# In the last two wide blocks, layer 2 of half the tokens in seven products, with summed output weights through DRAM

## The chip, the cores and the metric

The kernel runs on one core of a Trainium2 chip. The metric is the device time of one execution in microseconds; lower is better. The kernel before took 1020.27 us (median of three runs, 1020.24 to 1021.65).

## The reference

Attention with random features, then a two-layer network over the 4608 tokens that come out of it, all in fp32:

```python
def phi(x):                       # x scaled by 64 ** -0.25
    proj = np.einsum('bhsd,md->bhsm', x, omega)
    h = proj - np.sum(x * x, axis=-1, keepdims=True) / 2.0
    return np.exp(h - np.max(h, axis=-1, keepdims=True)) / np.sqrt(m)
...
kv = np.einsum('bhsm,bhsd->bhmd', k_p, v);  z = np.sum(k_p, axis=2)
num = np.einsum('bhsm,bhmd->bhsd', q_p, kv)
den = np.einsum('bhsm,bhm->bhs', q_p, z)[..., None] + 1e-06
x = (num / den).transpose(0, 2, 1, 3).reshape(4608, 512)
...
h = x @ w_in                                         # 512 x 2048
g = np.where(h > 0, h, np.exp(np.minimum(h, 0)) - 1)  # ELU
out = g @ w_out                                      # 2048 x 512
```

There are 8 batches, 8 heads, 576 positions, 64 columns per head and 128 random features.

## The kernel before, in words

**Accuracy.** TensorE works on a reduced fp32 type, so every operand is kept as a high part and a low part (`xh`/`xl`, `w2h`/`w2l`, the two halves of a `gq` tile), and every product takes three matmuls: high by high, high by low, low by high.

**Stages.** Attention for pairs of heads runs beside the network: tokens that are finished go to DRAM (`xd`) and are fetched for the network when they are due. The network has 16 groups of 128 hidden features. The first 3072 tokens are done in blocks of 384: per group, layer 1 (L966 to L968), ELU (L975 to L987), layer 2 (L1000 to L1002). The last 1536 tokens are done in three **wide blocks** s = 0, 1, 2 of 512 tokens. A wide block has eight steps j, each for a pair of feature groups f = 2j and 2j + 1. Each step calls `fetch`, `wide1` and `wide2`.

**Layer 1 of a wide block** (`wide1`) takes seven products in place of eight (Strassen's method in Winograd's form over halves of the features, the inputs and the tokens). One product is six matmuls of 256 columns (L1223). Two PSUM banks called A and B collect them: A takes products 0, 5, 6 and 3 one on top of the other, and between them its partial sums are copied out to SBUF as c1, c2 and c3 (line 373 on ACT or 375 on DVE). B takes 1, 4 and 2, and its sums are added to these copies (L1246, DVE). The four results go through ELU (L1261 and L1266 on ACT, L1269 on DVE) and are split into `gq` tiles, a high part (copy, line 373 or 375) and a low part (subtraction, line 378, POOL or DVE). The two banks have one tag, "ph", with two slots, so A and B of a step take the slots that A and B of the step ahead give back.

**Layer 2 of a wide block** (`wide2`) is eight groups of three matmuls of 512 columns per step (L1312 to L1314), into one accumulator bank for each 128 tokens: `acc0` to `acc2` and one bank of the tag "pa". After the last step ACT copies each bank out (line 373) and SP stores it (L1327).

**Weights.** Layer 1 reads its weights from DRAM each step: three tiles `wp` of 512 KB (tag "w1c", three slots, L1191) and a half one, `wq` (L1196). Since a step uses all three slots, a `wp` load waits until TensorE has finished with the tile of the same number of the step ahead. The weights that Strassen's method needs summed are made ahead of time by `prepare` (L1036 to L1067), loaded as `rw`, summed on POOL, DVE and ACT, and stored to DRAM (`w1t`); some of them are made during block 0. The weights of layer 2 stay in SBUF.

**Order.** `Plan.order` is a list scheduler with costs, latencies, due times and buffer slots of its own; it fixes the order of the instructions on each engine when the program is built, and `Plan.issue` writes them in that order. SP issues all DMAs, strictly in its order, and waits for the condition of each before it goes on to the next. Constants at the head of the file set the due times and preferences (`STEP_S`, the length it assumes for a step; `LAG2`, how far layer 2 follows layer 1; `FETCH`, how early weights are due; `ALT`, which engine an operation may be given to).

## Time and profile before

| | us |
|---|---|
| median of three runs (device time) | 1020.27 |
| the profiled execution, device time | 1025.54 |
| its span, first to last instruction | 1023.8 |
| PE busy | 1002.9 |
| DVE busy | 743.4 |
| ACT busy | 708.0 |
| POOL busy | 542.2 |
| layer 1, blocks of 384: matmuls of L966, L967, L968, 512 each | 176.8, 172.7, 172.8 |
| layer 2, blocks of 384: matmuls of L1000, L1001, L1002, 384 each | 154.6, 151.3, 151.6 |

All times in the trace are microseconds from the start of the span. PE is TensorE's matmuls, PEld its weight loads, which have a track of their own. Matmuls are pipelined: the record of one is longer than the distance to the next, so that rates are read from distances between starts. In the profile a row of the view of lines is the engine's operation with "out<-in" by the names of the program, a count, busy time and the mean of one; rows of the timeline give start, duration, engine, line, operation, and in brackets the engine's idle time before it with what ended it. The three wide blocks stand at the end, from about 765 us on.

### The profile page before, as it was taken

To read this page: it belongs to the slowest core of one execution; us is meant where nothing else is said; L and a number is where in the kernel's file an instruction comes from. 1 tells how busy PE (TensorE), PEld (TensorE's weight loads), DVE (VectorE), ACT (ScalarE), POOL (GpSimd) and SP (SyncE) were. 2 spreads that over 40 slices of the span, in tenths; PEclk is the share of its full clock that TensorE was granted. 3 is DMA by queue.
4 is the path that set the end of the run, shared out by engine and by line. 5 is a ranking of instruction groups with operands and counts; after the bars stand their busy time and mean duration, and the time that the engine had idled before them with its cause. 6 is when DMAs were issued, how large, how long until landed. Compare 5 with 4: busy or idle time off the path is not lost. (4 is left out here: it accounts for less than half of the span.)

```text
span 1023.8 us, 23048 instructions
## 1 busy us (share of the span) xinstructions
PE 1002.9 (98%) x7374; PEld 882.3 (86%) x7374; DVE 743.4 (73%) x2799; ACT 708.0 (69%) x1879; POOL 542.2 (53%) x727
## 2 busy tenths in 40 slices
PE   7999999989999999999999999999999999999998
PEld 6888798878888888888888888888888989898897
DVE  5999977876778878888887888787675674345332
ACT  5999777777568788897788878875335555345443
POOL 0667676676457767776676766663003333323232
PEclk7999999999999999999999999999999999999999
DMA  6657677857766766676666867647979976666562
GB/s 172 184 182 217 233 265 251 256 175 238 236 244 200 228 221 218 201 250 201 218 220 201 250 186 231 204 153 213 332 269 346 311 276 205 197 204 194 192 183 82
DMA packets 91720, 226.17 MB, mean 221 GB/s; under 512 B 23056, under 2 KB 31952, under 8 KB 91600
## 3 DMA queue, kind: packets, MB, share of 16 engines
q1 hardware_dynamic: 91600, 224.70, 67.6%
q8 instruction: 59, 0.97, 0.4%
q14 instruction: 61, 0.50, 0.1%
HBM read 187.43 MB, written 37.22 MB: 219 GB/s over the span
## 5 line engine op out<-in xcount | busy, mean ns | idle before, releaser
L966 PE MATMUL ph<-xh,w1c 128*128 128x384 f32 x512 | 176.8, 345 | 5.7 <-DVE g L987 3.9
L967 PE MATMUL ph<-xl,w1c 128*128 128x384 f32 x512 | 172.7, 337 | 1.0 <-DVE xl L791 1.0
L968 PE MATMUL ph<-xh,w1c 128*128 128x384 f32 x512 | 172.8, 337 | 0.0
L378 POOL TENSOR_TENSOR gq<-y,gq 128x256 fp32r<-128x256 f32 x96 | 78.3, 832 | 171.3 <-ACT gq L373 97.7
L1000 PE MATMUL acc<-w2h,g 128*128 128x512 f32 x384 | 154.6, 403 | 0.1
L1002 PE MATMUL acc<-w2h,g 128*128 128x512 f32 x384 | 151.6, 395 | 0.0
L1001 PE MATMUL acc<-w2l,g 128*128 128x512 f32 x384 | 151.3, 394 | 0.0
L966 PEld LDWEIGHTS ph<-xh,w1c 128*128 128x128 f32 x512 | 96.6, 189 | 16.5 <-DVE g L987 6.6
L378 POOL TENSOR_TENSOR hq<-hq,den 128x512 f32<-128x512 f32 (+1 forms) x96 | 81.1, 853 | 46.2 <-DVE den L733 40.0
L967 PEld LDWEIGHTS ph<-xl,w1c 128*128 128x128 f32 x512 | 96.7, 189 | 4.0 <-DVE xl L791 1.4
L979 DVE SCALAR_TENSOR_TENSOR ph<-e,ph 128x384 f32<-128x384 f32 x128 | 71.2, 556 | 38.3 <-ACT e L976 37.5
L968 PEld LDWEIGHTS ph<-xh,w1c 128*128 128x128 f32 x512 | 96.6, 189 | 0.0
L975 ACT ACTIVATE e<-ph 128x384 f32<-128x384 f32 x128 | 62.6, 489 | 44.2 <-PE ph L968 43.0
L1002 PEld LDWEIGHTS acc<-w2h,g 128*128 128x128 f32 x384 | 72.1, 188 | 17.1
L724 DVE CUSTOM_DVE_ANT_0 junk<-hq,pz 128x128 f32<-128x128 f32 (+1 forms) x320 | 74.4, 279 | 15.7 <-PE pz L702 13.5
L1000 PEld LDWEIGHTS acc<-w2h,g 128*128 128x128 f32 x384 | 72.1, 188 | 15.7 <-issue 6.2
L375 DVE COPY c<-A 128x256 f32<-128x256 f32 x64 | 27.2, 425 | 74.2 <-PE A L1223 74.2
L458 ACT ACTIVATE hk<-hk,nbk 128x128 f32<-128x128 f32 x216 | 68.4, 390 | 17.2 <-POOL nbk L564 16.8
L1001 PEld LDWEIGHTS acc<-w2l,g 128*128 128x128 f32 x384 | 72.2, 188 | 8.1
L378 POOL TENSOR_TENSOR tk<-xk,tk 64x576 fp32r<-64x576 f32 x44 | 62.7, 1425 | 29.4 <-ACT tk L373 13.4
L458 ACT ACTIVATE hq<-hq,nbq 128x128 f32<-128x128 f32 x216 | 68.4, 391 | 11.1 <-POOL nbq L564 10.5
L1313 PE MATMUL acs<-w2l,gq 128*128 128x512 f32 x192 | 75.9, 395 | 0.0
(156 smaller groups left out, 2595.1 us busy)
## 6 DMA issues: line engine op xcount, KB each, us to landing
w1c<-w1s SPq DMA_DIRECT2D x112, 512.0 KB, 4.2
wp<-w1t SPq DMA_DIRECT2D x48, 512.0 KB, 3.9
raw_w<-in_w_dram SPq DMA_DIRECT2D x32, 512.0 KB, 4.2
xk<-in_kx_dram SPq DMA_DIRECT2D x24, 576.0 KB, 4.7
xq<-in_qx_dram SPq DMA_DIRECT2D x24, 576.0 KB, 4.6
wp<-w1s SPq DMA_DIRECT2D x24, 512.0 KB, 3.9
v<-in_v_dram SPq DMA_DIRECT2D x32, 325.0 KB, 3.3
out_dram<-o SPq DMA_DIRECT2D x36, 256.0 KB, 4.8
```

Source lines behind the costliest of these rows:

```text
L378: (nc.vector if e == "DVE" else nc.gpsimd).tensor_tensor(*args)
L458: nc.scalar.activation(h()[:, j, :], src(j), AF.Exp, bias=nb()[:, j:j + 1], scale=-1.0)
L724: nc.vector.tensor_tensor_reduce(out=junk()[r], in0=h()[r, j, :], in1=pz()[r, a * P:(a + 1) * P], scale=1.0, scalar=EPS, op0=ALU.mult, op1 ...
L966: nc.tensor.matmul(ph(), wh, xh[:, c, o:o + TB], start=(c == 0), stop=False)
L967: nc.tensor.matmul(ph(), wh, xl[:, c, o:o + TB], start=False, stop=False)
L968: nc.tensor.matmul(ph(), wl, xh[:, c, o:o + TB], start=False, stop=(c == NC - 1))
L975: op("ACT", act(TB, True), due, lambda: nc.scalar.activation(e(), ph(), AF.Relu, scale=-1.0), (p,), (e,))
L979: lambda: nc.vector.scalar_tensor_tensor(ph(), e(), -1.0, ph(), ALU.add, ALU.max), (p, e), (p,),
L1000: nc.tensor.matmul(a(), g[0]()[:, ts], w2h[:, f], start=(f == f0), stop=False)
L1001: nc.tensor.matmul(a(), g[0]()[:, ts], w2l[:, f], start=False, stop=False)
L1002: nc.tensor.matmul(a(), g[1]()[:, ts], w2h[:, f], start=False, stop=(f == f1 - 1))
L1313: nc.tensor.matmul(a(), g()[:, ts], w2l[:, f], start=False, stop=False)
```

## The change

In the wide blocks 1 and 2 (`NS2 = 1`), layer 2 is done by a new function `seven2` in place of `wide2`. Block 0 keeps `wide2`.

- **Products.** Of the 512 tokens of a block, the first half goes through layer 2 in seven products per step, over halves of the tokens, the two feature groups and halves of the 512 output columns. One product is three matmuls of 256 columns (L1473), 21 per step. The second half of the tokens goes the usual way: 12 matmuls of 512 columns (L1431 to L1433), into `acc2` and a bank `pc`. Each of the seven products adds up over the eight steps in its own half of a PSUM bank: products 1 and 2 share `acc0`, 5 and 6 share `acc1`, 4 and 3 share `pa`, 7 has half of `pb`.
- **Summed activations.** `elu` puts one ELU result into a tile `yv`, makes four sums of 128 columns from it and a second one (POOL or DVE), and splits them into a tile `gs`: one copy of 512 columns for the high part and one subtraction of 512 columns for the low part.
- **Summed output weights.** `prepare` is called a second time for each j. It sums `w2h` and `w2l` in SBUF into tiles `rv` (tag "h"; four operations of 512 columns, four of 256 and two copies of 512), and stores two tiles of 512 KB to a new DRAM array `w2t`, during block 0 and shortly before it. `summed_weights` loads them again in each step of blocks 1 and 2 (`tw`, two tiles of 512 KB, tags "raw" and "qh").
- **End of a block.** ACT copies product 1 out, seven additions on DVE (L1507) put the four output pieces together in the tiles of two stores, and two banks are copied out as before.
- **Constants.** All due times and preferences of the planner have new values, so that the order changes nearly everywhere: on PE from row 190 on.

In the code after the change, layer 1 of a wide block stands at L1269 (before L1223), its totals at L1292, ELU at L1313, L1318 and L1321, the usual layer 2 of block 0 at L1390 to L1392; the helpers of lines 373, 375 and 378 are at 377, 379 and 382. The stores of `prepare` are L1091, the loads of `wp` L1234, of `wq` L1239, of `rw` L1047.

```diff
--- before
+++ after
-STEP_SA, STEP_S = 11.9, 12.43
-LAG2 = 1.229
+STEP_SA, STEP_S = 9.83, 7.67
+LAG2 = 1.715
...
+NS2 = 1
-FETCH = 14.67
+FETCH = 8.89
...
+    w2t = dram.tile([NJP, 2, P, 2 * DM], F32, name="w2t")
...
-    def prepare(j, due):
+    def prepare(j, due, layer):
...
+                lambda x, e=e, f=f: tt(x, cols(e, 0, 2), w2h[:, f].bitcast(F32), w2l[:, f].bitcast(F32), ALU.add),
+                (("w2", f, "h"), ("w2", f, "l"), ("f", NBLK - 1, 8 + j)), [(r[e], k) for k in range(2)],
...
+        else:
+            add((0, 2), (0, 1), (0, 0), ALU.subtract, 1.0)
+            add((0, 3), (1, 1), (0, 2), ALU.subtract, 1.1)
+            add((1, 2), (1, 1), (0, 1), ALU.subtract, 1.2)
+            add((1, 3), (0, 3), (1, 0), ALU.subtract, 1.3)
...
+            op("SP", 500, due + 4 + e, lambda e=e: nc.sync.dma_start(store[j, e], cols(e, 0, 4)), [*head, *tail], ((nm, j, e),), P * 4096)
...
+    def summed_weights(s, j, due):
+        sums = [
+            Buf(sb, [P, 2 * 512], F32R, "raw", f"tw_{s}_{j}_0", 3), Buf(sb, [P, 10, M], F32R, "qh", f"tw_{s}_{j}_1", 2),
+        ]
+        gate = ("step", s, j - 2) if j > 1 else ("step", s - 1, j + 6) if s else ("f", NBLK - 1, 11 + 2 * j)
...
+        for e in range(2):
+            op(
+                "SP", 500, due - FETCH2 + 3 * e, lambda e=e: nc.sync.dma_start(at(e)[:, 0:1024].bitcast(F32), w2t[j, e]),
+                (("w2t", j, e), gate), (sums[e],), P * 4096,
+            )
+        tw[s, j] = {
...
+        if s >= NS2:
+            summed_weights(s, j, due)
...
+        if s >= NS2:
+            V = Buf(sb, [P, NV], F32, "v", f"yv_{s}_{j}", 2)
+            gs = gq[s, j] = Buf(sb, [P, 2 * S], F32R, "t", f"gs_{s}_{j}", 2)
...
+            sum_of(2, lambda: part(1), lambda: v()[:, P:TH], ALU.add, ((V, 1), y), 1.0)
+            sum_of(1, lambda: part(0), lambda: part(1), ALU.subtract, ((V, 0), (V, 1)), 1.1)
+            sum_of(3, lambda: part(2), lambda: part(0), ALU.subtract, ((V, 0), (V, 2)), 1.2)
+            sum_of(0, lambda: v()[:, 0:P], lambda: part(3), ALU.subtract, (y, (V, 3)), 1.3)
+            every = [(V, k) for k in range(4)]
+            op(
+                "ACT", act(4 * P), d + 1.4, lambda x: copy(x, gs()[:, 0:4 * P], V()[:, 0:4 * P]), every, ((gs, 0),),
+                alt=other("q_hi", "DVE", dve(4 * P, True)), port=True,
+            )
...
+                "POOL", pool(4 * P), d + 1.5,
+                lambda x: tt(x, gs()[:, 4 * P:8 * P], V()[:, 0:4 * P], gs()[:, 0:4 * P].bitcast(F32), ALU.subtract),
+                (*every, (gs, 0)), ((gs, 1),), alt=other("q_lo", "DVE", dve(4 * P)), port=True,
             )
...
+    HOME = {1: ("acc0", 0), 2: ("acc0", 1), 5: ("acc1", 0), 6: ("acc1", 1), 4: ("pa", 0), 3: ("pa", 1), 7: ("pb", 0)}
...
+                o = a()[:, half * TH:(half + 1) * TH]
+                for k, (b, c) in enumerate(((0, 0), (0, 1), (1, 0))):
+                    nc.tensor.matmul(o, x(b), w(c), start=start and k == 0, stop=stop and k == 2, skip_group_check=True)
...
+        product(1, tokens(0, 0), weight(0, 0))
+        usual(1)
+        product(2, tokens(1, 0), weight(1, 0))
+        product(4, tokens(1, 1), turned(4))
+        usual(0)
+        product(5, summed(2), turned(1))
+        product(6, summed(3), turned(2))
+        product(3, summed(0), weight(1, 1))
+        product(7, summed(1), turned(3))
+        if j < NJP - 1:
+            return
+        d = due + st * (LAG2 + 1)
+        c = Buf(sb, [P, 2, M], F32, "p2", f"cs_{s}", 4)
...
+        op("ACT", act(TH, True), d, lambda e: copy(e, flat(), m(1)[0]()), (m(1)[1],), (c,), alt=other("part", "DVE", dve(TH)))
+        add(piece(0, 0), m(2), cc, 0.1)
+        add(cc, m(6), cc, 0.2)
+        add(piece(1, 1), m(5), cc, 0.3)
+        add(piece(0, 1), m(3), piece(1, 1), 0.4)
+        add(cc, m(7), cc, 0.5)
+        add(piece(1, 0), cc, m(4), 0.6, ALU.subtract)
+        add(piece(1, 1), m(7), piece(1, 1), 0.7)
+        for z in range(2):
+            row = TOK0 + s * SB + z * P
+            op(
+                "SP", 500, d + 1, lambda z=z, row=row: nc.sync.dma_start(out[row:row + P], o[z]()), ((o[z], 0), (o[z], 1)), (),
+                P * DM * 4,
+            )
...
-        prepare(j, begin[NS0] + PREP0 + PREP * j)
+        prepare(j, begin[NS0] + PREP0 + PREP * j, 1)
+        prepare(j, begin[NS0] + PREPB + PREPC * j, 2)
...
-            wide2(s, j, begin[n] + j * pace, pace)
+            (seven2 if s >= NS2 else wide2)(s, j, begin[n] + j * pace, pace)
```

Three places of the order follow. First the order on PE in block 0, around the end of layer 1 of step 3: `A_3` and `B_3` are the two banks of step 3, `B_4` and `A_4` those of step 4, `wp_3_2` and `wq_3` the weights of the products 6 and 2, and of 3, `acs_*` the accumulators of layer 2. Before:

```order
L1223 MATMUL A_3_11729<-xh,wp_3_2_11718 128x256 x6
L1312 MATMUL acs_1_11532<-w2h,gq_2_10_11727 128x512
L1313 MATMUL acs_1_11532<-w2l,gq_2_10_11727 128x512
L1314 MATMUL acs_1_11532<-w2h,gq_2_10_11727 128x512
L1312 MATMUL acs_2_11564<-w2h,gq_2_01_11779 128x512
L1313 MATMUL acs_2_11564<-w2l,gq_2_01_11779 128x512
L1314 MATMUL acs_2_11564<-w2h,gq_2_01_11779 128x512
L1223 MATMUL A_3_11729<-xl,wq_3_11585 128x256 x6
L1223 MATMUL B_3_11740<-xh,wp_3_2_11718 128x256 x6
L1312 MATMUL acs_3_11539<-w2h,gq_2_01_11779 128x512
```

The same place after:

```order
L1269 MATMUL A_3_11847<-xh,wp_3_2_11823 128x256 x6
L1269 MATMUL A_3_11847<-xl,wq_3_11669 128x256 x6
L1269 MATMUL B_3_11838<-xh,wp_3_2_11823 128x256 x6
L1269 MATMUL B_4_11961<-xh,wp_4_0_11860 128x256 x6
L1269 MATMUL A_4_11972<-xh,wp_4_0_11860 128x256 x6
L1390 MATMUL acs_2_11655<-w2h,gq_3_11_11958 128x512
```

Before, two groups of layer 2 stood between product 6 and product 3 on bank A. After, product 3 follows product 6 at once, and bank B of step 4 follows the last product of bank B of step 3 at once.

Second the order on SP, in block 0, around the loads of step 2. `rw` and `rv` are the tiles of `prepare` for layer 1 and layer 2, `o_0_*` outputs. Before:

```order
L1191 DMA wp_1_2_11455<-w1t 128x1024
L1022 DMA out_dram<-o_0_0_11468 128x512
L1191 DMA wp_2_0_11489<-w1s 128x1024
L1022 DMA out_dram<-o_0_1_11497 128x512
L1191 DMA wp_2_1_11529<-w1t 128x1024
L1067 DMA w1t<-rw_0_11288 128x1024
L1067 DMA w1t<-rw_1_11412 128x1024
```

The same place after:

```order
L1091 DMA w2t<-rv_1_11405 128x1024
L1234 DMA wp_2_0_11570<-w1s 128x1024
L1234 DMA wp_2_1_11602<-w1t 128x1024
L1047 DMA rw_1_11618<-w1s 128x1024
L1091 DMA w2t<-rv_0_11554 128x1024
L1047 DMA rw_0_11643<-w1s 128x1024
L1234 DMA wp_2_2_11650<-w1t 128x1024
```

After, the stores of the new summed weights stand between the loads, each behind the engine that makes its tile.

Third the end of the program. Before, ACT's last operations, `acs_*` being the accumulators and `o_*` the tiles that go to DRAM:

```order
L373 COPY o_0_14226<-acs_0_13434 128x512
L373 CAST gq_7_01_14231<-y_7_01_14216 128x256
L373 COPY o_1_14241<-acs_1_13466 128x512
L373 COPY o_2_14247<-acs_2_13476 128x512
L373 COPY o_3_14250<-acs_3_13484 128x512
```

After, DVE's last operations (`acs_pa`, `acs_pb` and the two `acs_acc` hold the products, `cs` the copy of product 1):

```order
L1507 TENSOR_TENSOR o_0_14682<-acs_acc_13809,cs_14667 128x256
L1507 TENSOR_TENSOR cs_14667<-acs_acc_13923,cs_14667 128x256
L1507 TENSOR_TENSOR o_1_14696<-acs_acc_13923,cs_14667 128x256
L1507 TENSOR_TENSOR o_0_14682<-acs_pa,o_1_14696 128x256
L1507 TENSOR_TENSOR cs_14667<-acs_pb,cs_14667 128x256
L1507 TENSOR_TENSOR o_1_14696<-acs_pb,o_1_14696 128x256
L1507 TENSOR_TENSOR o_1_14696<-cs_14667,acs_pa 128x256
```

Where one copy followed the last matmul, a chain of additions now does, each on what the one ahead left.

More of the change, by code (lines that the diff above doesn't have):

```diff
@@ L1263, in negative @@
                     nc.vector.tensor_scalar(v(), src(), 0.0, -1.0, ALU.min, ALU.mult)
[L1265 to L1266 removed]
+            op("ACT", act(TH, psum), d, negative, (key,), ys, alt=other("neg", "DVE", dve(TH, not psum)), port=not psum)
+            op("ACT", act(TH), d + 0.2, lambda: nc.scalar.activation(v(), v(), AF.Exp, scale=-1.0), ys, ys)
             op(
                 "DVE", dve(TH), d + 0.6,
[L1269 removed]
+                lambda x: nc.vector.scalar_tensor_tensor(v(), v(), -1.0, src(), ALU.add, ALU.max), (*ys, key), ys,
                 alt=(), port=not psum,
```

173 lines of the change are left out of this document (134 added, 39 removed).

## Prediction

> **What bounds the kernel now.** I read the page first, then the windows, the waits of PE, the critical chain of a late step, and the timeline of it. The page:
>
> ```profile
> span 1023.8 us, 23048 instructions
> PE 1002.9 (98%) x7374; PEld 882.3 (86%) x7374; DVE 743.4 (73%) x2799; ACT 708.0 (69%) x1879; POOL 542.2 (53%) x727
> PE   7999999989999999999999999999999999999998
> DMA  6657677857766766676666867647979976666562
> ```
>
> PE is busy for 1002.9 of 1023.8 us. Only 20.9 us are idle, so the change has to pay in PE work. From the windows (us, PE, PEld, DVE, ACT, POOL, PE's clock, DMA share, GB/s):
>
> ```profile
> 0.00:20.00 20.00, 13.52 (x70) 12.88 (x71) 9.21 (x19) 9.22 (x25) 0.70 (x6) 0.78 0.67 191
> 766.00:840.00 74.00, 74.00 (x470) 66.71 (x469) 46.68 (x103) 40.74 (x106) 24.67 (x29) 1.00 0.88 316
> 764.00:794.00 30.00, 30.00 (x190) 26.93 (x189) 17.67 (x42) 15.07 (x39) 9.48 (x11) 1.00 0.91 336
> 770.00:790.00 20.00, 20.00 (x126) 17.94 (x125) 11.11 (x26) 11.43 (x29) 7.96 (x8) 1.00 0.98 362
> 775.00:780.00 5.00, 5.00 (x30) 4.33 (x30) 3.77 (x9) 2.76 (x7) 3.26 (x2) 1.00 1.03 415
> 854.00:938.00 84.00, 84.00 (x529) 75.46 (x528) 38.78 (x90) 40.78 (x109) 25.56 (x32) 1.00 0.63 201
> 1013.00:1024.00 11.00, 7.18 (x32) 5.49 (x30) 1.60 (x4) 5.12 (x12) 2.17 (x3) 1.00 0.26 96
> ```
>
> Of the idle time 6.5 us lie in the first 20 us and 3.8 in the last 11; the 10.6 us left lie between. In the wide blocks PE has none: 74.00 of 74.00 us in block 0, 84.00 of 84.00 in block 1. What stands between are single waits, the largest of which (engine, line, what it waited for; total, times, longest):
>
> ```profile
> PE ppk L488 <- ACT hk L458: 4.1, 1, 4.1
> PE ph L966 <- DVE g L987: 3.9, 5, 2.0
> ```
>
> Block 0 has another resource near its end, though: DMA is 0.88 busy there. Block 1 has room (0.63).
>
> **The change part by part.**
>
> *1. PE work saved.* Two pieces of the critical chain, one step apart (start, us, what):
>
> ```profile
> 917.23 0.70 PE A L1223 x6
> ...
> 927.74 0.70 PE A L1223 x6
> ```
>
> A step takes 927.74 - 917.23 = 10.51 us with no gap. The distances in the timeline give the share of layer 1:
>
> ```profile
> 930.37 0.87 PE L1223 MATMUL A<-xh,wp 128*128 128x256 f32 x6
> 931.08 0.87 PE L1223 MATMUL B<-xl,wp 128*128 128x256 f32 x6
> 931.27 0.42 DVE L375 COPY c<-A 128x256 f32<-128x256 f32 x1 [0.55 <-PE A L1223]
> 931.78 0.39 PE L1312 MATMUL acs<-w2h,gq 128*128 128x512 f32 x1
> 931.98 0.43 DVE L1246 TENSOR_TENSOR c<-B,c 128x256 f32<-128x256 f32 x1 [0.28 <-PE B L1223]
> ```
>
> Six matmuls of 256 columns advance PE by 0.705 us (930.37 to 931.08 to 931.78). Seven products are 4.93 us, and the eight groups of layer 2 share the other 5.58: 0.697 each, three matmuls of 512. Four such groups go and seven products of three matmuls of 256 come: 4 x 0.697 - 7 x 0.352 = 2.79 - 2.47 = 0.32 us a step. Sixteen steps: **-5.1 us**. That is little for a saving of an eighth of half of layer 2, but it is all there is.
>
> The matmuls are narrower, and 9 more per step need a weight load each. That costs nothing if loads stay hidden:
>
> ```profile
> L1223 PEld LDWEIGHTS A<-xh,wp 128*128 128x128 f32 x138 | 19.5, 188 | 2.1
> ```
>
> A load takes 188 ns and a matmul of 256 columns advances by 117 ns, yet six with six loads take only 0.705: the pace is that of the columns. [...]
>
> *2. The end.* Before, one copy follows the last matmul:
>
> ```profile
> 1019.79 0.39 PE L1314 MATMUL acs<-w2h,gq 128*128 128x512 f32 x1
> 1020.26 0.59 ACT L373 COPY o<-acs 128x512 f32<-128x512 f32 x1 [0.15 <-PE acs L1314]
> ...
> 1010.43 0.42 DVE L375 COPY c<-A 128x256 f32<-128x256 f32 x1 [2.75 <-PE A L1223]
> 1010.89 0.42 DVE L1246 TENSOR_TENSOR c<-B,c 128x256 f32<-128x256 f32 x1
> ```
>
> Call E the end of PE's pace, 1019.79 + 0.23 = 1020.02. The copy ended at 1020.85, E + 0.83. After, the last products are 5 and 6, then 3, then 7, which takes the last 0.35 us, 3 the 0.35 before it. The additions of 5 and 6 may start at E - 0.70 + 0.19 = E - 0.51 (0.19 is from 931.08 to DVE's start at 931.27). Six additions follow one another on DVE, 0.46 apart (1010.43 to 1010.89, the second needing the first): the last starts at E + 1.79 and ends at E + 2.21. The other five steps of DVE never wait for PE in that count. The store behind it is of the same size. So **+1.4 us**; it can't be much less, since the chain is serial, nor more than if all seven waited for the last product, 0.19 + 6 x 0.46 + 0.42 - 0.83 = 2.5.
>
> *3. Waits in block 0.* By the order on PE, three places have product 6 and product 3 back to back on bank A with the copy c3 between them (steps 1, 3 and 4), and at two places a bank is handed over with nothing between: `B_4` after the last of `B_3`, and `A` of block 1's first step after `B` of block 0's last. Before, at least two groups (1.40 us) stood in every such place of bank A. Each wait is priced by rows: PE's end to DVE's start 0.19, the copy 0.42, and from DVE's end back to PE:
>
> ```profile
> 201.10 0.56 DVE L987 TENSOR_TENSOR g<-ph,g 128x384 fp32r<-128x384 f32 x1
> ...
> 201.81 0.41 PE L966 MATMUL ph<-xh,w1c 128*128 128x384 f32 x1 [0.48 <-DVE g L987]
> ```
>
> ACT would take 0.37 for the copy:
>
> ```profile
> L373 ACT COPY c<-A 128x256 f32<-128x256 f32 x2 | 0.7, 374 | 0.6 <-PE A L1223 0.6
> ```
>
> 201.10 + 0.56 = 201.66 to 201.81 is 0.15. Together 0.76 us, five times 3.8. For `B_4` the total on which it waits stands on DVE behind the ELU maximum of the piece before, which waits for two operations of ACT; I add 0.2. Two more handovers of B have 0.70 us of cover for 0.76, and DVE has more to do in steps 1 to 4: 50 operations of 256 columns and 22 of 512, before 48 and 12. By these rows
>
> ```profile
> L378 DVE TENSOR_TENSOR rw<-rw 128x512 fp32r<-128x512 f32 x8 | 5.8, 764 | 0.1
> L378 DVE TENSOR_TENSOR rw<-rw 128x256 f32<-128x256 f32 x10 | 4.2, 416 | 0.1
> ```
>
> that is 50 x 0.42 + 22 x 0.76 = 37.7 of 42 us (four steps), before 29.3. DVE does not become the bound, but a copy that PE waits for can be queued behind a 0.76 us operation; I take 0.3 for both, with bounds 0 and 3 (0.76 at four waits). Sum of the block: 3.8 + 0.2 + 0.3 = **+4.3 us**, from 3.5 (copies on ACT and no queue) to 7.
>
> *4. DMA in block 0.* From the load of `wp` for step 1 to that for block 1's first step, SP's order moves 22.5 MB before and 28.3 MB after: eleven stores of `w2t`, and two loads of `tw`, come in, with some of the older transfers shifted. Before, the two loads issued at
>
> ```profile
> 766.58 0.32 SPq L1191 DMA_DIRECT2D wp<-w1s  x1
> ...
> 837.41 0.32 SPq L1191 DMA_DIRECT2D wp<-w1s  x1
> ```
>
> so 22.5 MB in 70.8 us, 318 GB/s at a share of 0.88. After, PE's work from the one to the other, counted over the order at the distances above (0.705 for six matmuls of 256, 0.697 for three of 512), is about 74 us, and 28.3 MB in 74 would be 382 GB/s. The windows show 316 at 0.88, 362 at 0.98, 415 at 1.03: per full share 359 to 403, with 369 over the longest full stretch. At 369, 28.3 MB take 76.7 us; the waits of part 3 stretch the 74 to 78.3. So DMA just fits: **0**. The bounds: at 403 it fits easily (0); at the 336 that the 30 us window sustained, it takes 84.2 us, +5.9 on top. [...]
>
> *5. Blocks 1 and 2.* Two loads of 512 KB more a step raise 201 GB/s by 1.05 MB / 10.2 us = 103, to about 305 with the shorter step, below the 362 seen. Counted so, loads have 7 us of PE work or more from release to use, but for two `wp` loads in the first two steps of block 1, with 4.2 and 5.3; a load lands in about 5.3 us when DMA is nearly full:
>
> ```profile
> wp<-w1t SPq DMA_DIRECT2D x6, 512.0 KB, 5.3
> ```
>
> The summed activations add about 4 operations of 128 columns and two of 512 a step, on POOL (25.56 of 84 busy), DVE (38.78) and ACT (40.78), with 12 us or more of PE work to their use. The narrowest handovers of A have 1.05 us of PE work for the 0.76 needed. **0**, at most 1.1 for the one load (5.3 - 4.2).
>
> *6. Before the wide blocks* the order is new as well. PE's work there is the same, and 10.6 us are idle. The new order could lose or save single waits such as the 4.1 us one; I see no sign for either: **0**, bounds -3 to +3.
>
> **Sum:** -5.1 + 1.4 + 4.3 + 0 + 0 + 0 = +0.6. The profiled execution (1025.54) was 5.3 us above the median, its span 3.5 above it; the sum is a difference within that span, and I carry it to the median, 1020.27 + 0.6 = **1020.9 us**.
>
> **The rivals.**
>
> *Faster.* The new order of the attention loses the long single waits: without the 4.1 us at L488 and with nothing in its place, and block 0 at its lower bound, -5.1 + 1.4 + 3.5 - 4.1 = -4.3; with 3 of the 4.1, -3.2, about **1017.1**. For it: 10.6 idle us lie there, in few waits. Against it: a new order has new waits, and nothing in it shows that they are fewer.
>
> *Slower: DMA becomes the bound in block 0.* The stores of `w2t` stand in SP's order between the loads of `wp`, and each waits for DVE, ACT or POOL; a load behind a late store is late too, and the queue then idles while it could move data. At 345 GB/s the stretch takes 82.0 us, 8.0 over 74, in place of 4.3: net +4.3, **1024.6**; at 336, 10.2 in place of 4.3: net +6.5. It lifts the sum over +2.04 from about 28.3 / (74 + 4.3 + 1.4) = 355 GB/s down. For it: 336 over 30 us, and one load of step 4 with 5.6 us from release to use. Against it: 362 over 20 us, and that PE's own waits give DMA time.
>
> *Weight loads no longer hidden.* Nine more loads a step at 188 ns, 16 steps: +27 us, about 1047 with the rest. The six-matmul distance of 0.705 speaks plainly against it. [...]
>
> *The change doesn't do what it says* is excluded by the order: 21 narrow and 12 wide matmuls stand in each step.
>
> **How the numbers follow.** A measurement of this kernel tells about 0.2%, 2.04 us, from no change. The forecast (within that of 1020.27) has 0.41, the faster rival 0.32, the DMA rival 0.26, unhidden loads 0.01. Faster by over 0.2% 0.32, within 0.41, slower 0.27. The likeliest case's own range is 1018.3 to 1022.3. The whole range goes down to the faster rival with all of the long wait gone (1020.27 - 4.3 = 1016.0) and up to the DMA rival at 345 GB/s, 1024.6, and 0.4 for part 5, 1025.0; outside lie the slower early order, DMA at 336, and the loads, about 2 in 10.
>
> **What would show it.** Right: PE's distance between steps in blocks 1 and 2 of 10.19 us with no idle time; the last addition of L1507 ending about 2.2 us after PE's pace; waits of PE of 0.7 to 1.0 us at c3 in steps 1, 3 and 4 of block 0, and at the two handovers; DMA above 0.95 in block 0 with `wp` landing before its use. Wrong: a step of 10.5 or more (loads show, or `tw` is late); waits of PE on DMA in block 0 (the slower rival); no idle time of PE in block 0 (part 3); or a difference of more than 1 us already there at the start of the wide blocks (part 6, and the faster rival where it is a gain).

## The result and the profile after

The changed kernel takes 1027.44 us (median of 20 runs, 1021.94 to 1031.09), the kernel before 1021.64 (20 runs, 1017.68 to 1028.48): a ratio of 1.0059, 95% interval 1.0043 to 1.0075. It is slower by 5.8 us, where +0.6 was forecast, and lies outside the range.

The page of after, span, engines and two rows of the slices:

```profile
span 1024.0 us, 23644 instructions
PE 998.2 (97%) x7518; PEld 882.9 (86%) x7518; DVE 775.5 (76%) x2828; ACT 745.8 (73%) x1997; POOL 585.3 (57%) x768
PE   7999999999999999999999999999999899999997
DMA  7656778777676767676676767469889997897973
```

PE is busy for less time than before, and still the span is no shorter: PE has become idle in the wide blocks. The windows of after (us, PE, PEld, DVE, ACT, POOL, clock, DMA share, GB/s) over most of block 0, and over a piece of blocks 1 and 2:

```profile
755.00:815.00 60.00, 54.83 (x329) 47.30 (x330) 48.42 (x95) 35.68 (x92) 22.19 (x23) 1.00 1.00 372
905.00:935.00 30.00, 29.20 (x215) 27.21 (x214) 19.70 (x43) 18.72 (x50) 11.93 (x14) 1.00 0.81 271
```

and the same 60 us of before:

```profile
755.00:815.00 60.00, 59.91 (x366) 53.32 (x365) 37.23 (x82) 30.89 (x77) 16.98 (x20) 1.00 0.86 311
```

In these 60 us PE was idle for 5, DVE was busy for 48 in place of 37, and the DMA share was 1.00. What PE waited for, in all (us, times, longest):

```profile
PE ppk L492 <- ACT hk L462: 3.0, 1, 3.0
PE A L1269 <- ACT c L377: 2.9, 5, 1.2
PE B L1269 <- DVE c L1292: 2.6, 3, 1.5
...
PE A L1269 <- DMA wp<-w1t: 0.6, 2, 0.4
```

The second, third and fourth row did not exist before.

**The lag.** A wait's row does not hold the whole loss, and two executions differ in their start (the two traces of before by 5.1 us of the lag in the table below). So I use one more number: the time at which a matmul starts, less PE's work ahead of it in the order, counted at the trace's pace (0.2325 us for 512 columns, 0.174 for 384, 0.1175 for 256). The attention's matmuls lie ahead of the wide blocks and count the same in every kernel. The lag grows by what PE loses, whether PE waits or its clock is lower; how exact it is shows in before, where no wait stands in the wide blocks and the lag only goes from 83.45 to 83.37. For product 3 of a step (the one with `wq`), step 0 of block 0 and step 0 of block 1, in after:

```profile
761.48 0.75 PE L1269 MATMUL A<-xl,wq 128*128 128x256 f32 x5
...
854.27 0.86 PE L1269 MATMUL A<-xh,wq 128*128 128x256 f32 x6
```

The work ahead is 686.44 and 770.55: the lag goes from 75.04 to 83.72, so block 0 loses 8.7 us. All kernels of this study in one table; "end" is the time from the end of PE's pace to the last copy or addition, "DVE" and "DMA" the busy time and share from 755 to 815 us:

| kernel | lag at block 0 | at block 1 | at block 2, step 7 | end | DVE | DMA | median us (before beside it) |
|---|---|---|---|---|---|---|---|
| before, first trace | 83.45 | 83.48 | 83.37 | 0.83 | 37.2 | 0.86 | 1021.64 |
| before, second trace | 78.33 | 78.44 | 78.33 | 0.83 | | | |
| after | 75.04 | 83.72 | 86.60 | 2.84 | 48.4 | 1.00 | 1027.44 (1021.64) |
| e1, no sums, no stores | 73.60 | 78.89 | 81.47 | 2.86 | 29.7 | 0.83 | 1022.81 (1020.85) |
| e2, no stores | 75.78 | 83.33 | 85.09 | 2.85 | 48.7 | 0.80 | 1025.51 (1020.85) |
| e3, other output buffer | 76.56 | 86.84 | 89.12 | 1.90 | | | 1026.19 (1020.85) |
| e4, constants alone | 75.58 | 76.23 | 77.03 | 1.67 | | | 1019.23 (1020.85) |
| e5, spaced | 74.26 | 83.56 | 84.83 | 1.89 | 47.7 | 1.00 | 1025.72 (1019.5) |
| e6, old constants | 76.88 | 97.83 | 103.88 | 4.31 | | | 1051.29 (1019.5) |
| e9, spaced, no sums or stores | 73.89 | 77.20 | 80.94 | 1.89 | 29.8 | 0.85 | 1019.44 (1021.29) |
| e14, spaced, no stores | 75.90 | 83.05 | 86.51 | 1.89 | 49.0 | 0.81 | 1022.68 (1019.72) |
| e15, spaced, no sums | 75.11 | 81.20 | 84.09 | 1.89 | 28.9 | 1.00 | 1021.38 (1019.72) |
| e8, block 2 alone | 77.44 | 82.85 | 84.20 | 1.89 | | | 1024.51 (1019.5) |
| e10, late sums | 72.34 | 84.85 | 91.34 | 1.89 | | | 1031.71 (1021.29) |
| e11, block 2 alone, sums in block 1 | 72.48 | 72.91 | 73.19 | 1.89 | 28.3 | 0.90 | 1016.83 (1021.29) |
| e12, late sums, own slots | 77.08 | 84.35 | 93.03 | 1.89 | | | 1027.13 (1018.02) |
| e13, spread sums, own slots | 75.78 | 86.04 | 89.81 | 1.89 | | | 1028.13 (1018.02) |

Each row is one execution. Some of them hold a stretch at half the clock in block 0, which PE's waits do not hold: 3.4 us of busy PE at a clock of 0.50 or 0.51 in e3 (from 814.1 us), e5 (808.2) and e13 (792.9), which is 1.7 us of lag each, and 6.3 us of busy PE in e12 (812.6), which is 3.1; e6 and e10 hold more. Without that stretch block 0 loses 8.6 us in e3 and 8.7 in after, whose orders are the same up to the end. So a block's loss can be compared between single traces once that stretch is taken off; the lag at block 0 cannot, as e7 shows below.

Before loses nothing in its wide blocks, in both traces. After against the second trace of before: lag at block 0 -3.3, block 0 +8.6, blocks 1 and 2 +3.0, end +2.0, PE's work -5.15 (931.49 against 936.64): +5.2, as the spans say (1024.0 and 1018.7) and near the medians' 5.8.

**Block 0, wait by wait.** The five places of the prediction, in after:

```profile
772.86 0.98 PE L1269 MATMUL A<-xl,wq 128*128 128x256 f32 x6 [0.46 <-ACT c L377]
800.26 0.99 PE L1269 MATMUL A<-xl,wq 128*128 128x256 f32 x6 [0.46 <-ACT c L377]
802.53 0.98 PE L1269 MATMUL B<-xh,wp 128*128 128x256 f32 x6 [0.60 <-DVE c L1292]
810.35 0.98 PE L1269 MATMUL A<-xl,wq 128*128 128x256 f32 x6 [1.21 <-ACT c L377]
847.85 0.97 PE L1269 MATMUL A<-xl,wp 128*128 128x256 f32 x6 [0.52 <-DVE c L1292]
```

With the part that the bracket leaves out (start less the pace of what was ahead) they cost 0.62, 0.62, 0.73, 1.38 and 0.67: 4.0 us, the forecast sum. But there are two more, of 1.63 and 0.74 by the same count:

```profile
763.81 0.98 PE L1269 MATMUL B<-xh,wp 128*128 128x256 f32 x6 [1.46 <-DVE c L1292]
811.91 0.98 PE L1269 MATMUL B<-xh,wp 128*128 128x256 f32 x6 [0.58 <-DVE c L1292]
```

The other 2.2 us of block 0 are in steps of 0.3 or less: 0.2 to 0.3 at the first matmul of three groups of layer 2, and 0.1 behind each wait, where a second matmul also starts late.

What DVE and POOL did ahead of the wait at 763.81, where PE needs the total of L1292:

```profile
758.80 0.69 DVE L382 TENSOR_TENSOR rw<-rw 128x512 f32<-128x512 f32 x1 [1.60 <-DMA rw<-w1s]
...
760.42 2.99 DVE L382 TENSOR_TENSOR rw<-rw 128x256 f32<-128x256 f32 x3
...
761.07 1.46 POOL L382 TENSOR_TENSOR rv<-rv 128x512 fp32r<-128x512 f32 x1
...
763.34 0.41 DVE L1292 TENSOR_TENSOR c<-B,c 128x256 f32<-128x256 f32 x1
```

DVE first waits 1.60 us for a load, then three sums of 256 columns take 2.99 us while POOL works beside them (three of them alone take 1.25, by the 416 ns in before), and the total stands behind them in DVE's queue. Ahead of the waits at 810.35 and 811.91:

```profile
808.27 0.87 PE L1269 MATMUL A<-xh,wp 128*128 128x256 f32 x6
...
808.44 1.88 DVE L382 TENSOR_TENSOR rw<-rw 128x512 fp32r<-128x512 f32 x3
...
808.89 1.13 ACT L377 CAST rv<-rv 128x512 fp32r<-128x512 f32 x2
809.94 0.36 ACT L377 COPY c<-A 128x256 f32<-128x256 f32 x1
810.24 1.28 DVE L382 TENSOR_TENSOR rv<-rv 128x512 fp32r<-128x512 f32 x2
...
811.45 0.41 DVE L1292 TENSOR_TENSOR c<-B,c 128x256 f32<-128x256 f32 x1
```

Product 6 is through PE at 808.98; its copy starts at 809.94, behind two copies of the new sums on ACT, and the total behind two subtractions on DVE. So it is not the room beside a copy alone that decides, but also what stands ahead of it in its engine's queue.

### The profile page after: what moved, and what is told of

Same layout as the page of the kernel before. It is cut to its first block, busy times and chain, and to the rows that moved or that the text cites. A ratio compares the mean times of both kernels' runs of the same rounds, so it can differ in the third digit from the quotient of the medians.

```text
span 1024.0 us, 23644 instructions
## 1 busy us (share of the span) xinstructions
PE 998.2 (97%) x7518; PEld 882.9 (86%) x7518; DVE 775.5 (76%) x2828; ACT 745.8 (73%) x1997; POOL 585.3 (57%) x768
## 4 chain that ended last, share of the span: by engine, by line
PE 75%; DVE 10%; DMA 4%; issue 4%; ACT 4%; POOL 3%; SPq 0%; DVEq 0%; POOLq 0%; ACTq 0%
PE ph L970 8%; PE acc L1004 7%; PE ph L972 7%; PE ph L971 7%; PE acc L1006 7%; PE acc L1005 7%; PE A L1269 5%; PE B L1269 4%; PE pkv L610 3%; PE pn L830 3%; PE ppq L542 3%; PE ppk L542 2%; PE acs_acc L1473 2%; DMA wp<-w1t 1%; DVE u_w L915 1%
## 5 line engine op out<-in xcount | busy, mean ns | idle before, releaser
L382 POOL TENSOR_TENSOR gq<-y,gq 128x256 fp32r<-128x256 f32 x80 | 67.0, 841 | 127.2 <-ACT gq L377 116.2
L970 PEld LDWEIGHTS ph<-xh,w1c 128*128 128x128 f32 x512 | 96.2, 188 | 12.5 <-DVE g L991 4.6
L382 POOL TENSOR_TENSOR tq<-xq,tq 64x576 fp32r<-64x576 f32 x46 | 65.8, 1431 | 22.1 <-DVE nbk L556 7.2
L382 POOL TENSOR_TENSOR tk<-xk,tk 64x576 fp32r<-64x576 f32 x47 | 66.9, 1423 | 13.2 <-ACT tk L377 6.1
L991 DVE TENSOR_TENSOR g<-ph,g 128x384 fp32r<-128x384 f32 x128 | 70.6, 551 | 4.2
```

The source lines that it names most:

```text
L382: (nc.vector if e == "DVE" else nc.gpsimd).tensor_tensor(*args)
L970: nc.tensor.matmul(ph(), wh, xh[:, c, o:o + TB], start=(c == 0), stop=False)
L991: lambda: nc.vector.tensor_tensor(g[1]()[:, 0:TB], ph(), g[0]()[:, 0:TB].bitcast(F32), ALU.subtract),
```

## The experiments

**What the preparation costs in this order: e1 and e2.** The order of everything else is kept. In e1 the sums and their stores are left out, in e2 the stores alone; in both `tw` reads other weights of the same size.

```diff
+        def op(eng, ns, due, fn, *a, **k):
+            if layer == 2:                 # e2: if layer == 2 and eng == "SP"
+                fn = lambda *x: None
+            pl.op(eng, ns, due, fn, *a, **k)
...
-nc.sync.dma_start(at(e)[:, 0:1024].bitcast(F32), w2t[j, e])
+nc.sync.dma_start(at(e)[:, 0:1024].bitcast(F32), w1t[j, e])
```

> The changed kernel with the sums of the output weights neither made nor stored (the loads tw read the summed layer 1 weights of the same size instead); every other instruction keeps its place in the order. In the changed kernel PE loses 8.0 us in block 0 and 2.2 in blocks 1 and 2, counted as the distance between matmul starts beyond their pace. Theory A, the order: the five places where a copy stands between two products with no work beside it cost about 0.65 each whatever else runs, 3.3 us stay in block 0 and the other 4.7 go, since they are DVE operations delayed by the preparation; time 4 to 5 us below the changed kernel. Theory B, load alone: nearly all of the 8.0 goes, 7 to 8 us below. Theory C, order alone: 7 or more stay, time within 1 us.

Measured: 1022.81 us, ratio to before 1.0018 (0.9996 to 1.0039), 4.6 below after, or 3.8 with each taken against its own before. The five places keep 0.62, 0.63, 0.74, 0.62 and 0.67, 3.3 us, as theory A has it. Block 0 loses 5.3 by the lag, though, not 3.3: the steps of 0.3 or less stay too and make the other 2.0. So there are two costs, one of the order, 5.3, and one of the preparation, 3.4. In blocks 1 and 2 the loss is 2.6 in place of 2.9: it does not come from the preparation.

> The changed kernel with the sums made but their stores to DRAM left out (tw reads the summed layer 1 weights); the order is kept. If DVE and POOL are what PE waits behind, 7 or more of the 8.0 us of block 0 stay and the time is within 1.5 us of the changed kernel. If DMA and the SP queue are (5.8 of 28.3 MB in the tight stretch go), block 0 falls to 3 to 5 us, as without the preparation.

Measured: 1025.51, ratio 1.0051 (1.0034 to 1.0068). Block 0 loses 7.6 in place of 8.7. So the stores are the smaller part in this order, 1.1 of 3.4, as the first of the two forecasts has it. The way they act shows in the wait at 763.81, which is here

```profile
763.44 0.97 PE L1274 MATMUL B<-xh,wp 128*128 128x256 f32 x6 [0.36 <-DVE c L1297]
```

The loads of `rw` land earlier, so DVE is less late. From 755 to 815 us (median us to landing is the last column), after and e2:

```profile
rw<-w1s SPq DMA_DIRECT2D x6, 512.0 KB, 7.1
```

```profile
rw<-w1s SPq DMA_DIRECT2D x5, 512.0 KB, 5.8
```

**The end: e3.** The tiles `o_0` and `o_1` of the last block get a slot of tag "h"; the order is kept.

```diff
         o = [Buf(sb, [P, DM], F32, "u", f"o_{s}_{z}", 3) for z in range(2)]
+        if s == NSB - 1:
+            for b in o:
+                b.home = ("h", 4, [P, NJ, M])   # where the tile is taken from
```

> The changed kernel with the two output tiles that the additions at the end write put into another buffer; the order is kept. In the changed kernel the last addition ends 2.84 us after PE's pace ends. If the second addition waits for the landing of the store whose slot its tile takes, it starts at once here and the last addition ends 1.8 to 2.2 after PE's pace: 0.6 to 1.0 us less. If the chain of additions itself is that slow, 2.84 stays.

Measured: 1026.19, ratio 1.0047 (1.0029 to 1.0066). In after the second addition waits for a store of the other half, whose slot `o_1` takes (three slots, four output tiles):

```profile
1017.58 0.42 DVE L1507 TENSOR_TENSOR cs<-acs_acc,cs 128x256 f32<-128x256 f32 x1 [1.63 <-PE acs_acc L1473]
...
1017.74 0.52 PE L1473 MATMUL acs_pb<-tw,gs 128*128 128x256 f32 x3
1018.99 0.42 DVE L1507 TENSOR_TENSOR o<-acs_acc,cs 128x256 f32<-128x256 f32 x1 [0.98 <-DMA out_dram<-o]
...
1020.52 0.41 DVE L1507 TENSOR_TENSOR o<-cs,acs_pa 128x256 f32<-128x256 f32 x1
```

and in e3 it does not:

```profile
1020.11 0.42 DVE L1515 TENSOR_TENSOR cs<-acs_acc,cs 128x256 f32<-128x256 f32 x1 [1.63 <-PE acs_acc L1478]
1020.57 0.42 DVE L1515 TENSOR_TENSOR o<-acs_acc,cs 128x256 f32<-128x256 f32 x1
```

The end falls from 2.84 to 1.90: the 0.9 us are shown. All later kernels with seven products but e6 have this buffer.

**The part ahead of the wide blocks: e4, e6, e7.** e4 is the changed kernel with `NS2 = 3` and without `prepare(j, ..., 2)`; e6 has the constants of before with the seven products; e7 is before.

```diff
-NS2 = 1
+NS2 = 3
...
-        prepare(j, begin[NS0] + PREPB + PREPC * j, 2)
```

> The new constants with the usual layer 2 in all three blocks and no sums of output weights: PE's order equals that of the changed kernel up to row 3462, that is up to the wide blocks. If the new order ahead of the wide blocks is worth 3 us or so, as the ledger of the two profiles with their own distance from the medians says, the time is 2 to 5 us below the kernel before, with no waits of PE in the wide blocks. If that difference is only the spread between executions, it is within 1 us of it.

Measured: 1019.23, ratio 0.9987 (0.997 to 1.0004): 1.6 us below before, less than the 2 to 5 forecast and not clear of nothing. PE loses 1.4 us in the wide blocks, where no wait was forecast, and 0.8 more at the end. If the median holds, the part ahead of them gives 3 to 4.

> The change with the constants of the kernel before (the new ones keep their values only where the kernel before has none): PE's order equals that of before up to the wide blocks. Its order has eight places with too little work between products of bank A, so block 0 loses 6 to 10 us. If the new order ahead of the wide blocks is worth 3 to 4 us, as the run with the new constants alone has it, the time is 1028 to 1033, 1 to 5 above the changed kernel. If the early order is worth nothing, it is 1025 to 1028.

Measured: 1051.29, ratio 1.0307 (1.028 to 1.0334), far above what either theory had, so it tells nothing of the part ahead. With the due times of before block 0 loses 21 us in place of the 6 to 10 forecast, and blocks 1 and 2 another 6. Which waits make them stays open.

> The kernel before, for a second trace of it. In its first trace the wide blocks begin 7.9 us later than with the new constants, counted against PE's work done; by the medians the early part is worth 3 to 4. If the rest was the clock of that one execution (0.78 over the first 20 us, where others show 0.91 to 1.00), the wide blocks begin 3 to 5 us earlier here. If not, 7 to 8 us stay.

Measured: 1020.51 us in one execution. The lag at block 0 is 78.33 in place of 83.45: 5.1 us of the first trace were that execution's own. Executions of one order differ at the start. These are the same 16 matmuls of the attention in the two traces of before, and in e1 and e8, which have the new order:

```profile
12.25 3.79 PE L488 MATMUL ppk<-of,xk 128*128 128x128 f32 x16 [4.13 <-ACT hk L458]
...
10.35 3.73 PE L488 MATMUL ppk<-of,xk 128*128 128x128 f32 x16 [0.59 <-ACT hk L458]
...
10.67 2.19 PE L492 MATMUL ppk<-of,xk 128*128 128x128 f32 x16 [0.87 <-ACT hk L462]
...
12.06 3.79 PE L497 MATMUL ppk<-of,xk 128*128 128x128 f32 x16 [2.25 <-ACT hk L467]
```

They start up to 1.9 us apart and take 2.19 us or 3.7 to 3.8. The clock in the windows does not tell these apart: over the first 20 us it is 0.78 in the first trace, but 1.00 in the other three. And the wait of 4.1 us, which the prediction read as a wait of the order, is 0.6 in the second trace of before and between 0.8 and 3.5 in the 14 traces of the new order. The lag at block 0 is 76.9 (e6), 78.3 and 83.5 in the three traces with the old order ahead of the wide blocks, and 72.3 to 77.4 in the 14 with the new, so two single traces do not give the gain.

What the order itself gains shows behind the start. From 40 to 745 us all waits of PE come to 8.5, 8.8 and 9.1 us in the three traces of the old order, and to 4.7 to 6.8, 5.6 in the mean, in the 14 of the new: about 3 us, as the median of e4 has it. Most of that is layer 1 of the blocks of 384 waiting for DVE (L966 before, for `g`): 3.9, 4.8 and 5.2 us with the old order, 2.0 to 3.2 with the new.

**Room in the order: e5, e9, e14, e15.** Five PE tasks of block 0 are moved back in the order, so that each place has 0.70 us of other products.

```diff
+MOVES = (          # what, behind what
+    (('group', 0, 0, 1, 3), ('product', 0, 1, 6)),
+    (('group', 0, 3, 0, 1), ('product', 0, 3, 6)),
+    (('group', 0, 3, 0, 0), ('product', 0, 3, 2)),
+    (('group', 0, 3, 1, 1), ('product', 0, 4, 6)),
+    (('product', 0, 7, 3), ('product', 0, 7, 2)),
+)
```

> The changed kernel with the output tiles of the end in the other buffer, and five PE tasks of block 0 moved back in the order, so that every copy that a product or a bank of step 1, 3 and 4 and of the first step of block 1 waits for has 0.70 us of other products beside it. If the back-to-back places are what costs (theory A), the 3.3 us of the five places go, and with them the 0.9 us that two of them cost in the product behind; block 0 loses 3 to 4.5 us in place of 8.0, the end 1.9 in place of 2.84, time 1021.5 to 1023.5. If PE waits at these places for a DVE or ACT that is late anyway, the waits move to the next product and the sum of block 0 stays above 6.5; time 1025 or more.

Measured: 1025.72, ratio 1.0053 (1.003 to 1.0076). Block 0 loses 9.3 us, 7.6 without the stretch at half the clock. Theory A fails here: the waits moved. The largest is now at product 6 of step 4:

```profile
807.70 1.18 PE L1289 MATMUL A<-xh,wp 128*128 128x256 f32 x6 [2.29 <-ACT rv L397]
```

ACT's `rv` is the name that the profile gives, but no product reads it. The load of these weights was issued at 799.65, and loads of `wp` took up to 7.9 us there, which is 807.55: PE waits for the load. e15 names it.

> The order with the spaced places and the other output buffer, and without the sums of the output weights and their stores (tw reads the summed layer 1 weights). Theory D, formed on the runs so far: in steps 0 to 4 of block 0 DVE and POOL have more to do than time, so with the preparation the waits only move when the places are spaced; without it the places are what is left. Then block 0 falls from 3.9 (without the preparation alone) to under 1.3 us and the time to 1018 to 1020. If the places do not matter in either case, block 0 stays at 3.5 to 4 and the time at 1021 to 1023.

Measured: 1019.44, ratio 0.999 (0.9975 to 1.0006). Without the preparation the room is worth 2.0 us in block 0 (3.3 in place of 5.3, against e1), and the kernel is not told from before. The time is in the range of theory D, the loss is not: it had under 1.3. The places do matter, but they are not all that is left: 3.3 us stay in block 0 and 3.7 in blocks 1 and 2, in a kernel with no preparation at all.

> The order with the spaced places and the other output buffer; the sums of the output weights are made, but not stored (tw reads the summed layer 1 weights). With the stores the lag of PE grows by 9.3 us in block 0 in this order, its largest wait, 2.45 us at product 6 of step 4, starting 7.9 us after the load of its weights was issued. If the stores are what this order waits for (loads land late, by the DMA queue), that wait goes and block 0 loses 3 to 5 us, time 1020 to 1022.5. If DVE and ACT are, block 0 still loses 7 or more and the time is 1024 or more.

Measured: 1022.68, ratio 1.0038 (1.0018 to 1.0059). Block 0 loses 7.2, as the second forecast has it, though the time is below its 1024. The wait at product 6 of step 4 is gone, the one on ACT behind it is there:

```profile
809.26 0.97 PE L1294 MATMUL A<-xl,wq 128*128 128x256 f32 x6 [1.23 <-ACT c L397]
```

> The same order with all stores and loads, but without the sums: the stores write 512 KB of the unsummed output weights at the same places of the queue. If DMA alone is what the spaced order waits for, block 0 loses 7 us or more and the time is 1024 or more. If the sums on DVE and ACT are needed for the loss, it is 2 to 4.5 us, time 1019.5 to 1022.

The sums are left out; the stores write unsummed weights.

```diff
-cols(e, 0, 4)
+cols(e, 0, 4) if layer == 1 else w2h[:, 2 * j:2 * j + 2].rearrange("p f x -> p (f x)").bitcast(F32)
```

Measured: 1021.38, ratio 1.0011 (0.9996 to 1.0025). Block 0 loses 6.1, between the two forecasts, and here PE waits for the weights:

```profile
806.85 0.94 PE L1294 MATMUL A<-xh,wp 128*128 128x256 f32 x6 [1.42 <-DMA wp<-w1t]
```

The four kernels have one order and lose, without the stretch at half the clock in e5, 7.6 us (sums and stores), 7.2 (sums), 6.1 (stores) and 3.3 (neither) in block 0. The sums alone cost 7.2 - 3.3 = 3.9 us, the stores alone 6.1 - 3.3 = 2.8, and both together 7.6 - 3.3 = 4.3, or 6.0 if that stretch is counted as a cost of the wait ahead of it. So either half of the preparation is enough to make PE wait, each in its own way: the sums through DVE's and ACT's queues, the stores through a full DMA queue. By the medians, each against its own before (+6.2, +3.0, +1.7 and -1.9), the sums alone cost 4.8, the stores alone 3.5 and both 8.1, each uncertain by some 3 us. Whether the two halves add up stays open.

**The preparation elsewhere: e8, e10 to e13.** e8 has `NS2 = 2` and late due times for the sums (with `STEP_SA` 11.45, `FETCH` 11.89). e10 to e13 hold the sums back by what they depend on:

```diff
-(("w2", f, "h"), ("w2", f, "l"), ("f", NBLK - 1, 8 + j))
+(("w2", f, "h"), ("w2", f, "l"), ("step", *GATE[j]))
```

> Seven products in block 2 alone, with the sums of the output weights made from late in block 0 through block 1, where DVE and POOL have room, and the output tiles of the end in the other buffer. PE's work falls by 2.6 in place of 5.1 us. Its order has two places in block 0 with nothing beside a copy and two with 0.70. If preparation beside a full block 0 and the order there are the cause, block 0 loses 1.5 to 2.5 us, and the time is 1017.5 to 1020.5, below the kernel before. If the seven products cost as such (the reloads, the additions at the end), it is within 1 us of the kernel before or above it.

Measured: 1024.51, ratio 1.0047 (1.0031 to 1.0064). A miss, and no test of the theory: a due time only ranks work, so the planner still put the sums nearly where it had put them, 72 of their 80 operations ahead of 820 us in the trace, and block 0 loses 5.4 us. The lag of 77.44 ahead of it is this execution's start (the last of the four rows above): PE's order there is that of after.

> The whole change in blocks 1 and 2, with the other output buffer, but the sums of the output weights held back until PE has begun steps 3, 4, 5, 5, 6 and 7 of block 0 and 0 and 1 of block 1 (j = 0 to 7), behind the preparation for layer 1; the order follows from that, with one place left that has nothing beside a copy. Theory D: block 0 loses under 2.5 in place of 8 us and the time is 1018.5 to 1021.5. If the amount of preparation costs the same wherever it stands beside wide blocks, blocks 0 and 1 together still lose 7 or more, and the time is 1024 to 1027.

Measured: 1031.71, ratio 1.0119 (1.0096 to 1.0143). A miss, beyond both forecasts. Up to step 5 block 0 lost 1.7 us, and 12.5 by its end: PE waited 3.2 us for the inputs of block 1, and its clock fell, by which it lost about 4 more (half of the 7.84 us that PE is busy from 846.6 to 856.9, at a clock of 0.50):

```profile
845.00:855.00 10.00, 6.40 (x25) 5.70 (x26) 6.62 (x12) 5.80 (x13) 0.00 (x0) 0.58 0.51 187
```

> Seven products in block 2 alone, the sums held back until block 1 (j from step j of block 1 on), with the other output buffer; no place is left without other work beside a copy. PE's work falls by 2.6 us. Theory D: blocks 0 and 1 lose under 1.5 us in all, the end 1.1 more than before, and with the early gain of about 4 the time is 1014.5 to 1017.5, below both kernels. If preparation beside a wide block costs wherever it stands, block 1 loses 4 or more and the time is 1019 to 1022.

Measured: 1016.83, ratio 0.9966 (0.9946 to 0.9986), faster than both kernels and in the range of theory D. Blocks 0 and 1 lose 0.4 us, block 2 another 0.3. The one wait that the profile shows in the wide blocks is

```profile
815.32 0.98 PE L1277 MATMUL B<-xh,wp 128*128 128x256 f32 x6 [0.17 <-DVE c L1300]
```

> The whole change in blocks 1 and 2 again, the sums held back as in the run with the late sums (steps 2, 3, 3, 4, 5, 6, 7 of block 0 and 0 of block 1), but their tiles in the buffer t, which is free in block 0, so that they no longer take the slots of the input tiles xw of block 1. If the 10 us lost at the end of block 0 there came from the late inputs of block 1, they go: blocks 0 and 1 lose under 3 us and the time is 1014 to 1018. If DVE cannot make the sums beside block 0 at all, the loss stays above 7 and the time above 1021.

> The same with the sums one step of block 0 apart from step 1 on (two at step 5), so that they overlap more of the preparation for layer 1 (steps 0 to 3). If what PE waits for is set by how much DVE and POOL have to do in a step, blocks 0 and 1 lose 1 to 4 us more than with the later sums. If only the slots mattered, the two runs are alike within 1 us.

Measured: 1027.13, ratio 1.0085 (1.0059 to 1.0111), and 1028.13, ratio 1.0094 (1.007 to 1.0118). The first forecast of e12 fails and the second holds. Where e10 lost 10.2 us, from step 7 of block 0 to the first step of block 1, e12 loses 1.5, so the late inputs may well have been the cause there; but the sums stand earlier in e12 as well, and 5.7 us are lost from step 4 to step 5 in their place (3.1 of them at half the clock). Block 0 loses 7.3 in e12 and 10.3 in e13, blocks 0 and 1 together 14.3 and 13.2. So e13 did not lose the 1 to 4 us more that a load set by the step alone would give; without the stretches at half the clock (3.1 and 1.7 in e12, 1.7 in e13) it is 9.5 and 11.5, and how much the place matters stays open. No place in block 0 that was tried will do. The tiles have slots of their own here, but two where there were four, and in e13 a clump begins with them:

```profile
783.89 0.69 DVE L390 TENSOR_TENSOR rv<-w2h,w2l 128x512 f32<-128x512 f32 x1 [2.62 <-DMA w2t<-rv]
...
789.81 1.88 DVE L390 TENSOR_TENSOR rw<-rw 128x512 fp32r<-128x512 f32 x3
...
791.61 0.41 DVE L1329 SCALAR_TENSOR_TENSOR y<-y,A 128x256 f32<-128x256 f32 x1
...
792.07 0.98 PE L1277 MATMUL B<-xh,wp 128*128 128x256 f32 x6 [4.22 <-DVE y L1329]
```

DVE waits 2.62 us until a store has left a tile free, the sums of both layers pile up behind that, and the maximum of the ELU that PE needs comes last.

## Why the prediction was wrong, point by point

| term | forecast | measured |
|---|---|---|
| 1, PE work | -5.1 | -5.15 |
| 2, the end | +1.4 | +2.0 |
| 3 and 4, block 0 | +4.3 + 0 | +8.6 |
| 5, blocks 1 and 2 | 0 | +3.0 |
| 6, ahead of the wide blocks | 0 | -3.3 |
| sum | +0.6 | +5.2 |

Block 0 and blocks 1 and 2 were forecast 7.3 us too low together, the end 0.6; the gain of term 6, which the forecast had at nothing, hides 3.3 of that. The level was low as well: the 1020.27 that the forecast starts from is a median of three, and 20 runs have 1021.64.

*1* was right: product matmuls of 256 columns keep the pace of their columns, 0.1175 us each, and weight loads of 188 ns stay hidden (from step 0 to step 5 of block 1 the lag of after stays between 83.69 and 83.74).

*2* had the chain of additions right (1.4 less 0.3, since additions that wait for nothing follow 0.33 apart: 1.90 - 0.83 = 1.07 in e3). It left out the slot: the prediction counted "the other five steps of DVE never wait for PE", and did not ask whether they wait for a store. That is 0.9 us, which e3 shows.

*3* is the step that failed. The five places came out at 4.0 for 4.0. The last part, "I take 0.3 for both, with bounds 0 and 3", is the mis-sized term: 8.6 less 4.0 is 4.6. It was read from a mean ("37.7 of 42 us ... DVE does not become the bound"). DVE's work did come out as counted: from the start of step 1 to that of step 5 (767.82 to 814.82) it is busy for 37.2 us. But a queue in order needs only a clump: a load that lands 1.6 us late, then six sums, then the total that PE waits for (1.63 us); or five more of these operations, then the total (0.74). And I priced the copies on DVE or ACT as if those were free, while the change puts copies of the new sums on ACT's queue as well, so that one of the five places costs 1.38 where e1 has 0.62. The rest of the 4.6, 2.2 us, are the steps of 0.3 or less, which the prediction has no term for; they stay without the preparation. So 3.4 of the 8.6 us are shown to be the preparation's (e1), most of it by the sums (e2), and 5.3 the order's.

*4*: PE waited for no load in block 0, and DMA moved 372 GB/s over 60 us, so "DMA just fits" held. But a DMA that just fits is not free: loads of `rw` took 7.1 us where e2 had 5.8, and that made DVE late; e2 puts 1.1 us on it in this order, and in the other the stores cost between 0.4 (e5 without its stretch at half the clock, against e14) and 2.8 (e15 against e9). The slower rival had the place right (stores among the loads in SP's order) and the way only in part: the queue did not idle, its share was 1.00, and in after DVE is what comes late (1.46 us at 763.81), in e15 the weights (1.42 us at 806.85).

*5* is a second term put at nothing: 3.0. In e1, without the preparation, it is 2.6, and in e4, with the usual layer 2, 0.8: so most of it comes with the seven products themselves. Two copies come late, at 907.80 and 921.96; ahead of the second stands work of ACT that in turn waits for DVE. And two `wp` loads come late, where PE's work to their use was counted but not what DMA does at a share of 0.87 to 0.90 (968 to 983 and 945 to 962 us):

```profile
921.96 0.98 PE L1269 MATMUL A<-xh,wq 128*128 128x256 f32 x6 [0.53 <-ACT c L377]
...
961.85 0.94 PE L1269 MATMUL A<-xl,wp 128*128 128x256 f32 x6 [0.17 <-DMA wp<-w1t]
...
982.22 0.92 PE L1269 MATMUL A<-xl,wp 128*128 128x256 f32 x6 [0.41 <-DMA wp<-w1t]
```

*6*: the new order ahead of the wide blocks does gain, as the faster rival had it, but not where that rival looked. Its 4.1 us at L488 were mostly that one execution's start. The gain of about 3 us is in the waits of layer 1 for DVE, in the blocks of 384, which the prediction lists as the second of the largest waits (3.9 us) and does not price. The 3.3 in the table is the difference of two single traces.

So both signs that the prediction weighed were there, and the loss is the larger. The preparation is not the whole of it: e9 has none, and its wide blocks lose 3.3 + 3.7 us and 1.1 at the end, more than the 5.1 of work that is saved; that it is level with before in time it owes to the order ahead. In one block the seven products pay, though not much. e11 has its sums beside block 1, where no sums for layer 1 are made, and lies 0.34% below before (0.14 to 0.54), 4.5 us by the medians. About 3 of these are the order ahead; in the wide blocks it saves 2.6 us of work, loses 0.7 and ends 1.1 later, so 0.8 are left. Against e4, which has that order and no seven products, it is 2.8 us lower, each against its own before, with an uncertainty as large. A kernel with two blocks of seven products that beats before was not found: wherever their sums stood in block 0, block 0 lost 7 us or more, in part by the order and at half the clock.

## What to carry to other kernels

When work is taken from the bound engine by giving more to others, a share of busy time says little (here DVE was busy for 37.2 us of the 47.0 from step 1 to step 5, 37.7 forecast, and block 0 lost 8.6 us): look in the order at what stands ahead of each operation that the bound engine waits for, on that operation's own queue, and at what the first of those waits for. Count slots too: an addition can wait for the store of a tile that it has nothing to do with, here for 0.98 us. And compare several traces of a kernel before reading a difference of a few us from one, or a wait as the order's own.
